# One attention block with a gate: the two loads of the gate's weights move from SyncE's queue to GpSimd's

## The chip, the cores and the metric

The kernel runs on one core of a Trainium2 chip. The metric is the device time of one execution in microseconds; before, it is 1303.49 us, the median of three runs (1303.37 to 1303.68). All data is fp32.

## The reference

One decode step for two batch rows of 512 numbers: a layer norm, attention over a cache of 32768 keys and values for 8 key heads (each shared by 4 query heads, of 128 numbers), and a gate, which is a small two-layer network on the same normed input.

```python
def reference(A_x, A_k_cache, A_v_cache, A_wq, A_wo, B_x, B_w1, B_b1, B_w2, B_b2):
    def _A_ref(x, k_cache, v_cache, wq, wo):
        ...
        q = (lambda x, *d: x.transpose(*d))((x @ wq).reshape(B, Sq, Hq, Dh), 0, 2, 1, 3)
        ...
        scores = jnp.einsum("bhqd,bhkd->bhqk", q, k) * (Dh ** -0.5)
        p = _softmax(scores, axis=-1)
        o = jnp.einsum("bhqk,bhkd->bhqd", p, v)
        ...
    def _B_ref(x, w1, b1, w2, b2):
        h = jnp.einsum("bsd,df->bsf", x, w1) + b1
        ...
        r = jnp.where(h > zero, h, zero)
        h = r * r
        out = jnp.einsum("bsf,fd->bsd", h, w2) + b2
        return out
    x = A_x
    xn = _layernorm(x, axis=-1)
    s = _A_ref(xn, A_k_cache, A_v_cache, A_wq, A_wo)
    g = _silu(_B_ref(xn, B_w1, B_b1, B_w2, B_b2))
    return x + s * g
```

The sizes: `wq` is 512 x 4096 (8.39 MB), `w1` 512 x 1792 and `w2` 1792 x 512 (3.67 MB each), `wo` 4096 x 512 (8.39 MB). Keys and values are 16 pairs of batch and key head, 16.78 MB of keys and 16.78 MB of values each.

## The kernel before

A sequence is one of the 16 pairs of batch and key head. Its keys come in two loads of 8.39 MB, its values in two more; in each, every partition gets one piece of 64 KB. Keys go into `kring`, a ring of three slots of 64 rows per partition (4.19 MB each over all partitions), values into `vbuf`, one buffer of the size of two slots. DVE transposes the keys 32 x 32 into two buffers `kt` (L309, two instructions for each slot of keys, 4.41 us each), TensorE makes scores from them (`te_scores`, L270), ACT copies the scores out, the softmax follows, and TensorE multiplies with the values (`te_values`, L280). Three hardware loops, on PE, ACT and DVE, run over the sequences 1 to 15; sequence 0 is written out ahead of them. The order on each engine is the order of the program text, and engines wait for each other by semaphores.

All big loads are issued by SyncE (`load(SP, ...)`, L84 in the profile), in the order of the text. A load that has to wait for its buffer holds up all loads behind it in that queue. Ahead of the loops the order is as follows; `transposed(q)` means that DVE is done with the q-th slot of keys.

1. `wq` into `vbuf`, which is not yet needed for values; then the first K load (two slots), then one half of the second K load (slot 2).
2. `w1` into the lower part of `vbuf`, when the query projection has read `wq` (`q_done[1]`).
3. The other half of the second K load (`k1_in`, slot 1), when slot 1 is transposed (`transposed(0)`).
4. `w2` into the upper part of `vbuf`, with the same mark as `w1`.
5. The two halves of the third K load, one after `transposed(1)`, one after `transposed(2)`.
6. The first V load, after the gate's second layer (`mlp_done`); then the fourth K load, and so on, K and V in turn.

GpSimd makes some constants in the first 2 us, then waits for the queries and makes `qz` (`set_q`, L246), the masked query that the scores of a sequence need, once for each sequence.

On TensorE and DVE the gate stands between the scores of the first slots: scores of slots 0 and 1, first layer (L375 to L378, waits for `w1`), its squared ReLU on DVE (L381 to L385), scores of slot 2 (the first half of the second K load that is used, `k1_in`), second layer (L393, waits for `w2`), scores of slot 3. DVE keeps the same order, so it transposes the keys of `k1_in` only after the first layer.

Of the kernel before, what the change touches and what calls it, by code (L numbers as in the profile page):

```python
# [11 lines left out]
P = 128  # L12
# [40 lines left out]
def gqa_decode_kernel(nc, x, kc, vc, wq, wo, w1, b1, w2, b2, out):  # L53
# [20 lines left out]
    def bank(name, n=1):  # L74
# [3 lines left out]
    SP, ACT, DVE, POOL, TE = (Lane(nc, e, n) for e, n in (  # L78
        (nc.sync, "sp"), (nc.scalar, "act"), (nc.vector, "dve"), (nc.gpsimd, "pool"), (nc.tensor, "pe")))
    tensor, vector, scalar, gpsimd, sync = nc.tensor, nc.vector, nc.scalar, nc.gpsimd, nc.sync  # L80

    def load(lane, dst, src, sem, *marks):
        lane.wait(*marks)
        return sem.after(lane.eng.dma_start(dst, src))  # L84

    def dma(name):
        return Count(nc, name, 16)
# [32 lines left out]
    def transposed(q):  # L120
        return KT[1].at(q + 1)

    def load_k_half(m, i, *marks):
        c = k_order(m)[i][1]
        return load(SP, k_slot(2 * m + i), k_rows(m)[:, c * SLOT:(c + 1) * SLOT], k_sems[m % 2], *marks)
# [7 lines left out]
    w1_t = vflat[:, 0:ND * F].rearrange("p (d f) -> p d f", d=ND)  # L133
    w2_t = vflat[:, ND * F:ND * F + FJ * D].rearrange("p (j e) -> p j e", j=FJ)
# [70 lines left out]
    q_done = []  # L205
# [5 lines left out]
                                             wq_t[:, d, cc * 512:(cc + 1) * 512], start=(d == 0), stop=(d == ND - 1)))  # L211
        q_done.append(t)

    w1_in = load(SP, w1_t, w1.rearrange("(p d) f -> p d f", p=P), dma("w1"), q_done[1])
    k1_in = load_k_half(1, 0, transposed(0))
    w2_in = load(SP, w2_t, w2.rearrange("(p j) e -> p j e", p=P), dma("w2"), q_done[1])
    load_k_half(2, 1, transposed(1))
    load_k_half(2, 0, transposed(2))

# [396 lines left out]
```

## Time and profile before

| | |
|---|---|
| median of the runs | 1303.49 us |
| span of the profiled execution | 1302.6 us |
| DVE busy | 619.0 us (48%) |
| PE busy | 639.7 us (49%) |
| ACT, GpSimd busy | 128.6 us, 11.9 us |
| read from HBM | 561.01 MB |

The span is the time from the first to the last instruction of one profiled execution; the median is of runs without a profile, and 0.9 us longer. In the profile, DMA share is the mean busy share of the core's 16 DMA engines. A row of the timeline has a start, a duration, the engine, the line in the kernel, the operation and its operands, and in brackets how long the engine was idle before and what ended that. A DMA's row on SPq or ACTq is its issue; the time at which it has landed is seen by who waits for it. The chain of work that ended last is followed back from the last instruction; a piece "DMA" in it runs from the issue to the landing.

### The profile page before, as it was taken

Reading aid. Unit: us, or ns where it says so; the run is one execution under the profiler, and the core shown is the slowest. Engines: PE = TensorE matmul, PEld = TensorE weight load, DVE = VectorE, ACT = ScalarE, POOL = GpSimd, SP = SyncE. Lnnn points to the kernel's source line nnn. Section 1 sums busy time; section 2 is a strip of 40 time slices with the busy share of each in tenths; the row PEclk is TensorE's granted clock in tenths of the full one; section 3 lists DMA queues with packets and bytes.
Section 4 is the critical chain, followed back from the end, with each engine's and each line's share of the span. In section 5 each row is a group of like instructions: output and inputs, shape, how many; then the busy total and the mean of one; then the engine's idle time right before and its main releaser. Section 6 shows DMA issues by size and latency. Waiting matters only on the chain.

```text
span 1302.6 us, 10806 instructions
## 1 busy us (share of the span) xinstructions
PE 639.7 (49%) x4710; PEld 175.6 (13%) x4710; DVE 619.0 (48%) x305; ACT 128.6 (10%) x262; POOL 11.9 (1%) x41
## 2 busy tenths in 40 slices
PE   3555444555535455544536543444653444554368
PEld 1111110111101011110101111111110111111014
DVE  2565553436555344655435555343655534455410
ACT  0111011111001011000111101011100101101010
POOL 0000000000000000000000000000000000000000
PEclk9778677878767787777788777678877778877789
DMA  9999999999999999999999999999999999999998
GB/s 419 418 448 423 441 427 435 431 437 433 431 437 427 443 427 441 429 441 427 439 427 437 433 431 437 427 443 427 441 429 441 427 439 427 439 431 429 441 425 356
DMA packets 10703, 561.14 MB, mean 431 GB/s; under 512 B 1199, under 2 KB 1219, under 8 KB 1478
## 3 DMA queue, kind: packets, MB, share of 16 engines
q1 hardware_dynamic: 10656, 560.99, 99.6%
q8 instruction: 6, 0.10, 0.0%
q10 hardware_dynamic: 38, 0.02, 0.0%
q14 instruction: 3, 0.02, 0.0%
HBM read 561.01 MB, written 0.00 MB: 431 GB/s over the span
## 4 chain that ended last, share of the span: by engine, by line
DMA 77%; DVE 12%; issue 10%; PE 1%; SPq 0%; DVEq 0%
DMA kring<-in_A_k_cache 73%; DVE kt L309 12%; DMA kring<-in_A_v_cache 2%; DMA kring<-in_A_wo 2%; PE o_ps L280 1%; PE acc_ps L533 0%; PE pj_ps L540 0%; SPq L84 0%; DVEq L308 0%; PE acc_ps L411 0%
## 5 line engine op out<-in xcount | busy, mean ns | idle before, releaser
L309 DVE STREAM_TRANSPOSE kt<-kring 128x4096 f32<-128x4096 f32 x128 | 557.6, 4414 | 449.4 <-DMA kring<-in_A_k_cache 449.4
L270 PE MATMUL ps_s<-kt,qz 128*32 128x512 f32 x2048 | 333.5, 779 | 603.4 <-DVE kt L309 603.4
L280 PE MATMUL o_ps<-vbuf,pTh 128*16 128x512 f32 x1984 | 227.5, 612 | 1.8 <-DMA vbuf<-in_A_v_cache 1.8
L270 PEld LDWEIGHTS ps_s<-kt,qz 128*32 128x32 f32 x2048 | 67.8, 128 | 845.1 <-issue 669.9
L333 ACT ACTIVATE sc<-ps_s,halves 128x512 f32<-128x512 f32 x64 | 46.6, 729 | 866.5 <-PE ps_s L270 866.5
L280 PEld LDWEIGHTS o_ps<-vbuf,pTh 128*16 128x16 f32 x1984 | 57.8, 101 | 178.0 <-issue 158.6
L343 ACT COPY pTh<-pT_ps 64x256 f32<-64x256 f32 x128 | 46.9, 366 | 39.6 <-PE pT_ps L299 21.6
L315 DVE CUSTOM_DVE_ANT_0 sc<-sc 128x1024 f32<-128x1024 f32 x16 | 19.6, 1225 | 54.9 <-ACT sc L333 54.9
L318 DVE CUSTOM_DVE_ANT_0 junk<-mx_ps,other 128x128 f32<-128x128 f32 x16 | 4.7, 292 | 82.1 <-PE mx_ps L288 82.1
L336 ACT ACTIVATE sc<-sc,nm 128x1024 f32<-128x1024 f32 x16 | 18.4, 1149 | 108.9 <-DVE nm L318 108.9
L328 DVE TENSOR_REDUCE hr<-fin_ps 128x4 f32<-128x64 f32 x16 | 3.6, 225 | 48.5 <-PE fin_ps L292 48.5
L292 PE MATMUL fin_ps<-ident,o_sb 128*128 128x128 f32 x64 | 10.5, 286 | 17.4 <-DVE o_sb L485 17.2
L348 ACT COPY o_sb<-o_ps 128x512 f32<-128x512 f32 x15 | 8.8, 586 | 97.2 <-PE o_ps L280 97.2
L299 PE MATMUL pT_ps<-ident,sc 128*128 128x128 f32 x128 | 17.5, 282 | 0.0
L299 PEld LDWEIGHTS pT_ps<-ident,sc 128*128 128x128 f32 x128 | 15.3, 147 | 0.0
L280 PE MATMUL o_ps<-kring,pTh 128*16 128x512 f32 x64 | 9.3, 749 | 9.0 <-DMA kring<-in_A_v_cache 9.0
L493 POOL COPY oT<-ho 128x4 f32<-128x4 f32 x15 | 2.8, 188 | 1147.2 <-DVE ho L329 1147.2
L210 PE MATMUL pT_ps<-vbuf,xnT 128*32 128x512 f32 x64 | 8.5, 693 | 7.4 <-DMA vbuf<-in_A_wq 7.4
L227 DVE COPY kt<-pT_ps 128x512 f32<-128x512 f32 x8 | 5.0, 683 | 13.2 <-PE pT_ps L210 13.2
L540 PE MATMUL pj_ps<-ident 128*128 128x128 f32 x88 | 10.8, 278 | 0.0
L540 PEld LDWEIGHTS pj_ps<-ident 128*128 128x128 f32 x88 | 10.1, 192 | 1.9 <-issue 1.9
L485 DVE TENSOR_TENSOR o_sb<-o_sb,o_ps 128x512 f32<-128x512 f32 x15 | 10.2, 682 | 0.0
(90 smaller groups left out, 105.5 us busy)
## 6 DMA issues: line engine op xcount, KB each, us to landing
kring<-in_A_k_cache SPq DMA_DIRECT2D x4, 4096.0 KB, 23.8
vbuf<-in_B_w SPq DMA_DIRECT2D x2, 3584.0 KB, 28.5
kring<-in_A_wo SPq DMA_DIRECT2D x1, 4096.0 KB, 41.2
kring<-in_A_wo SPq DMA_DIRECT2D x1, 2304.0 KB, 25.5
kring<-in_A_wo SPq DMA_DIRECT2D x1, 1024.0 KB, 27.6
kring<-in_A_wo SPq DMA_DIRECT2D x1, 512.0 KB, 28.4
vbuf<-in_A_v_cache SPq DMA_DIRECT2D x31, 30.1
kring<-in_A_k_cache SPq DMA_DIRECT2D x30, 29.8
```

The source lines that it names most:

```text
L270: i = tensor.matmul(ps_s[32 * g:32 * g + 32, :], qz[:, 2 * y + e, :], kt[y][:, g * NO:(g + 1) * NO, 32 * e:32 * e + 32], start=(y == 0 and ...
L280: mm_ = tensor.matmul(o_ps[32 * g:32 * g + 16, :], pTh[:, 2 * g + c, 2 * i:2 * i + 2, :, :].rearrange("p o y h -> p (o y h)"), vt[:, lo:lo ...
L292: t = tensor.transpose(fin_ps[:, i * P:(i + 1) * P], o_sb[:, i * DH:(i + 1) * DH], ident)
L299: t = tensor.transpose(pT_ps[:, k // 4, (k % 4) * P:(k % 4 + 1) * P], p[:, k * P:(k + 1) * P], ident)
L309: KT[y].after(vector.transpose(kt[y], k_slot(q)[:, :, 64 * y:64 * y + 64]))
L315: return DVE(lambda: vector.tensor_tensor_reduce(scf[0], scf[0], scf[1], 1.0, -3.4e38, ALU.add, ALU.max, rm), mark, on=on)
L333: ACT(lambda: scalar.mul(sc[c][:, :, :, u], ps_s.rearrange("p (o w) -> p o w", w=32), halves[:, c:c + 1]), *marks, on=EV)
L336: return ACT(lambda: scalar.activation(scf[0], scf[0], AF.Exp, bias=nm, scale=SCALE, accum_out=l), mark, on=on)
L343: i = scalar.copy(pTh[64 * a:64 * a + 64, :, :, y, :], v[64 * y:64 * y + 64, :, :, a0, a, :])
L348: scalar.copy(o_sb, o_ps).then_inc(OE.sem, 32)
L485: DVE(lambda: vector.tensor_add(o_sb, o_sb, o_ps), on=OSR)
L540: tensor.matmul(pj_ps[:, 0:P], ident, ident, start=True, stop=True)
```

## The change

Both loads of the gate's weights are issued by GpSimd. Their waits, sources, destinations and semaphores stay the same.

```diff
-    w1_in = load(SP, w1_t, w1.rearrange("(p d) f -> p d f", p=P), dma("w1"), q_done[1])
+    w1_in = load(POOL, w1_t, w1.rearrange("(p d) f -> p d f", p=P), dma("w1"), q_done[1])
     k1_in = load_k_half(1, 0, transposed(0))
-    w2_in = load(SP, w2_t, w2.rearrange("(p j) e -> p j e", p=P), dma("w2"), q_done[1])
+    w2_in = load(POOL, w2_t, w2.rearrange("(p j) e -> p j e", p=P), dma("w2"), q_done[1])
     load_k_half(2, 1, transposed(1))
     load_k_half(2, 0, transposed(2))
```

On SyncE, after the first K load and one half of the second, the order was this and is now this (`in_B_w1` and `in_B_w2` are the gate's weights, `kt_1` is DVE's count of transposed slots, `pe` TensorE's count of instructions done):

```order
 L84 DMA kring<-in_A_k_cache 128x16384
 L84 DMA kring<-in_A_k_cache 128x8192
-L84 DMA vbuf<-in_B_w1 128x7168 [waits pe]
-L84 DMA kring<-in_A_k_cache 128x8192 [waits kt_1]
-L84 DMA vbuf<-in_B_w2 128x7168 [waits pe]
-L84 DMA kring<-in_A_k_cache 128x8192 [waits kt_1] x2
+L84 DMA kring<-in_A_k_cache 128x8192 [waits kt_1] x3
 L84 DMA vbuf<-in_A_v_cache 128x16384 [waits pe]
 L84 DMA kring<-in_A_k_cache 128x16384 [waits kt_1]
```

The three half loads of keys that wait for DVE now follow each other with nothing between them.

On GpSimd the two loads come between its constants and the first `qz`:

```order
 L155 MEMSET ones 128x128
 L157 COPY sel4<-ident 4x128 [waits pool]
+L84 DMA vbuf<-in_B_w1 128x7168 [waits pe]
+L84 DMA vbuf<-in_B_w2 128x7168 [waits pe]
 L246 TENSOR_TENSOR qz<-qT,bm 128x128 [waits dve,act]
 L422 MEMSET oR 128x1024 [waits dve]
```

Both wait for the same count of TensorE, and `qz` stands behind them. TensorE, DVE and ACT keep their order.

## Rows read from the trace of the kernel before

**Rows 1.** of the page: span, DMA share in 40 slices, bytes, the chain's shares

```profile
span 1302.6 us, 10806 instructions
...
DMA  9999999999999999999999999999999999999998
...
HBM read 561.01 MB, written 0.00 MB: 431 GB/s over the span
...
DMA 77%; DVE 12%; issue 10%; PE 1%; SPq 0%; DVEq 0%
```

**Rows 2.** Windows: us, busy time of each engine (count), granted clock, DMA share, GB/s

```profile
40.00:100.00 60.00, 31.71 (x216) 8.95 (x216) 40.65 (x20) 8.07 (x12) 1.39 (x2) 0.73 1.01 435
100.00:1000.00 900.00, 435.93 (x3130) 109.62 (x3130) 442.48 (x194) 87.06 (x174) 6.79 (x22) 0.77 1.00 433
0.00:43.20 43.20, 13.29 (x100) 6.63 (x100) 10.77 (x25) 4.25 (x18) 1.68 (x10) 0.96 0.97 413
```

**Rows 3.** Timeline of SyncE's queue: start us, us, what (all of L84)

```profile
0.74 0.38 SPq L84 DMA_DIRECT2D vbuf<-in_A_wq  x1
...
31.55 0.33 SPq L84 DMA_DIRECT2D vbuf<-in_B_w  x1
...
52.48 0.43 SPq L84 DMA_DIRECT2D vbuf<-in_B_w  x1
...
85.66 0.33 SPq L84 DMA_DIRECT2D vbuf<-in_A_v_cache  x1
```

**Rows 4.** Chain of work that ended last: start us, us, what

```profile
43.30 8.78 DVE kt L309 x2
52.10 19.03 DMA kring<-in_A_k_cache
71.14 0.03 issue
...
71.23 8.78 DVE kt L309 x2
80.03 19.05 DMA kring<-in_A_k_cache
...
99.17 0.12 DVE kt L309
...
107.97 29.91 DMA kring<-in_A_k_cache
...
146.77 29.82 DMA kring<-in_A_k_cache
...
185.49 29.79 DMA kring<-in_A_k_cache
```

**Rows 5.** Timeline, first 48 us, engines: start us, us, what [idle before]

```profile
1.43 1.22 ACTq L84 DMA_DIRECT2D kt<-in_A_x  x1
...
10.34 0.69 DVE L188 TENSOR_REDUCE st<-kt 128x1 f32<-128x512 f32 x1 [7.33 <-DMA kt<-in_A_x]
...
22.90 8.52 PE L210 MATMUL pT_ps<-vbuf,xnT 128*32 128x512 f32 x64 [7.38 <-DMA vbuf<-in_A_wq]
...
28.12 2.48 DVE L227 COPY kt<-pT_ps 128x512 f32<-128x512 f32 x4 [12.28 <-PE pT_ps L210]
...
31.56 2.48 DVE L227 COPY kt<-pT_ps 128x512 f32<-128x512 f32 x4 [0.95 <-PE pT_ps L210]
...
35.56 0.46 POOL L246 TENSOR_TENSOR qz<-qT,bm 128x128 f32<-128x128 f32 x1 [33.58 <-ACT qT L235]
...
47.90 3.64 PE L270 MATMUL ps_s<-kt,qz 128*32 128x512 f32 x16 [12.83 <-DVE kt L309]
```

**Rows 6.** Timeline, the gate's first layer

```profile
62.64 1.01 PE L375 MATMUL pj_ps<-b1t,sel 4*128 4x448 f32 x2
...
68.56 0.65 DVE L385 STREAM_TRANSPOSE hT<-oR 128x448 f32<-128x448 f32 x1
```

**Rows 7.** Timeline, the output's store

```profile
1300.79 0.63 ACTq L587 DMA_DIRECT2D out<-fin  x1
```

## The prediction

> **What bounds the kernel now.** I read the page first, for the share of the DMA engines: its slices are full from the first to the last, 561.01 MB are read at 431 GB/s, and the chain of work that ended last is 77% DMA [rows 1]. No compute engine is above half. I then asked whether full means full in the stretch that the change touches: from 40 to 100 us the DMA share is 1.01 at 435 GB/s, and from 100 to 1000 us 1.00 at 433 GB/s [rows 2]. So the sixteen DMA engines do not rest. The kernel's time is its bytes at that rate, plus a start and a tail, and a change that leaves the bytes alone can only add idle time to the DMA engines or change their rate.
>
> The rate as a duration: one K load and one V load, 8.39 MB each, take from one K issue of the loop to the next, 146.77 to 185.49 us, 38.72 us [rows 4]. That makes 19.36 us for an 8.39 MB load, 9.68 for a half K load (4.19 MB), and 8.47 for one of the two gate weights (3.67 MB, called w1 and w2 here). These figures give the landings of the early stretch. From the first K load's landing (DVE starts at 43.30) to that of the second half of the next one (71.23), the queue moved a K half, w1 and a K half: 9.68 + 8.47 + 9.68 = 27.83 us, and the chain shows 27.93 [rows 4]. The next stretch, 71.23 to 99.17, holds w2 and two K halves: the same sum, and 27.94 shown. So a landing there can be counted from the bytes that stand ahead of it.
>
> Third, the issues of SyncE's queue. In the loop a K load is issued when DVE has transposed the keys before it; issued at 107.97 it lands 29.91 us later [rows 4], so 10.5 us of other transfers were ahead of it. That is the cushion which keeps the engines fed. It neither grows nor shrinks from turn to turn, so time that the DMA engines once lose is not won back.
>
> **The change part by part.** I name the K loads in the order in which they land: k0 (8.39 MB), k1a, k1b, k2a, k2b (halves), then v0, k3.
>
> *Issue cost.* Two issues of 0.33 and 0.43 us leave SyncE [rows 3], where the next load behind each waits for DVE anyway: nothing is gained there. They come to GpSimd, which has stood idle for 33.58 us when it starts qz at 35.56 [rows 5]. No row shows a DMA that GpSimd issues. From below it costs what SyncE needs, 0.3 us each; from above I take the longest issue of the trace, 1.22 us on ACT [rows 5], for both 2.4 us from 31.55. That ends by 34.0, before qz's inputs are there; and TensorE needs qz only when the first half of k0 is transposed, at 47.9 [rows 5]. So it costs nothing, and stays free up to some 12 us.
>
> One rule speaks against GpSimd here. The Trainium skill (SBUF — State Buffer, the section "SBUF: two separate sides") says that while VectorE runs a two-port copy, GpSimd is locked out and cannot write the descriptors of a DMA that it issues. In this stretch DVE runs eight copies of which the second four fill 31.56 to 34.04 [rows 5]. By that rule w1 would start at 34 instead of 32 to 33. The sum below would be the same by either, because it hangs on the order of the last bytes only. Those copies read PSUM, while the section's example is a copy from SBUF to SBUF.
>
> *Order of the transfers.* This is the term that matters. Before, w1 stands behind k1a, and w2 behind k1b: both take their turn in one queue. Now both are let go together at 31.55 and run beside k0 and k1a. That two queues share an engine, rather than one waiting for the other's backlog, is seen at the start: ACT's 4 KB of x, issued at 1.43, after SyncE's first load at 0.74, are used at 10.34, long before that load's 22.90 [rows 3, 5]. So w1 and w2 take part of the rate from about 33 us on. If they alternate with SyncE's rows, row by row (64 KB for k0, which is 19.36/8 = 2.42 us; 28 KB for w1, 1.06 us; estimates from the rate), k0 with some four rows per engine still to come lands about 4 us later, at 47.4. k1b, waiting for k0's first transposes (52.10 − 43.30 = 8.8 us after [rows 4]), is issued at about 56.3 instead of 52.10, and k2a at about 65. Both are still ahead of need: the bytes up to w2 and k1a last until about 70. w1 lands before 60. The gate's first layer, held up to now by TensorE's scores, gets from 62.64 to 69.21 [rows 6], 6.6 us, and is done by about 74. All this hides.
>
> k1b now is the last of the six loads, where w2 used to follow it. It lands at 71.14 + 8.47 = 79.61. DVE then transposes it, and SyncE issues k2b: that was 80.03 − 71.14 = 8.89 us [rows 4], so at 88.50. Here the cover has gone. Before, w2 and k2a lay in the queue over these 8.89 us, 18.15 us of transfers. Now k2a alone lies there, 9.68 us, and v0 is no help: SyncE reaches it after k2b, and it waits for the second layer, 5.63 us later (85.66 − 80.03) [rows 3].
>
> 9.68 against 8.89 looks like enough, but an issue is not yet a transfer. With nothing in the queue ahead, the first load, issued at 0.74, is used at 22.90 [rows 3, 5]: 22.16 us, 2.80 more than 19.36. At the end, the 4 KB output is issued at 1300.79 and the span ends at 1302.6 [rows 1, 7]: 1.8 us. So k2b lands at 88.50 + 9.68 + 1.8 to 2.8, which is 100.0 to 101.0 instead of 99.08 [rows 4]: **0.9 to 1.9 us late**. I take the middle, 1.4, since k2b is large like the first load but meets a warm queue. After it the old cushion is back: v0, issued 94.1, finds k2b under way until about 100; k3 has v0's 19.36 us ahead of it. Nothing is won back, as shown above.
>
> *Rate while two queues run.* The only stretch with two queues at work ran at 413 GB/s, 0 to 43.20, with the start in it, against 433 later [rows 2]. If the 42 us of overlap ran at 413, they would lose 42 × 20/433 = 1.9 us. From below nothing, since a share of 1.00 leaves nothing to gain. The nearer row is the x load, whose wait cost k0's queue nothing visible; I take 0, and keep 1.9 for the range.
>
> Sum: span 1302.6 + 1.4 = 1304.0. The median of the runs is 1303.49, 0.9 above the profiled span; with the same 0.9 the time is 1304.9.
>
> **The rivals.**
>
> *No gap at all.* If w1 and w2 start late or get a smaller share, so that 2 us or more of w2 land behind k1b, k1b lands earlier and w2's rest covers the gap, as today. From 33 to 79.6 us 12.8 MB of K and 7.34 MB of weights pass, so this needs a share under about a third on the average, or a start after about 41 us. Then nothing is lost: 1303.5. For it: no row shows how fast GpSimd's queue starts or how it shares. Against it: alternation row by row, which lets w2 end about 5 us ahead of k1b.
>
> *Starved weights, slower.* If GpSimd's transfers go in pieces far smaller than 28 KB while SyncE's go in 64 KB, they get a few per cent and w1 lands only when SyncE's queue runs dry. That point is 99.08 − 9.68 − 8.47 = 80.9 us. DVE's program stands at the first layer, 6.6 us, until 87.5, and only then transposes k1b, 8.9 us; k2b is issued at 96.4 and lands at 107.9 to 108.9. That is 8.8 to 9.8 us late: 1312.3 to 1313.3, about 1312.8. It decides from the share at which w1 lands after 73 us: 3.67 of the 17.3 MB that pass from 33 to 73, a fifth. For it: the x load waited 8.9 us for 4 KB, so small pieces wait for large ones. Against it: each row of w1 is 28 KB in one piece, at both ends. The Trainium skill (DMA: Bandwidth & Descriptors, section "SWDGE vs HWDGE vs iDMA") gives a packet of such a queue as preferably at most 4096 B, which, if it held for these rows, would be this case; the same page's "The descriptor swizzle" counts one descriptor per 8 KB row, which speaks for whole rows. No run here shows either.
>
> *Faster.* Only if two queues lift the rate of the early stretch: from 33 to 43 us, 10 × 20/433 = 0.5 us, 1303.0. A gain beyond that has no source in a full DMA queue.
>
> **How the numbers follow.** A repeat of this kernel can tell about 0.2% from no change, 2.6 us. Forecast (gap of 0.9 to 1.9, with or without the lost rate) 0.65, of which 0.07 lies past 2.6 us; no gap 0.17; starved weights 0.14; faster 0.04, of which 0.02 beyond 2.6 us from things that I do not see. So faster 0.02, same 0.58 + 0.17 + 0.02 = 0.77, slower 0.07 + 0.14 = 0.21. The range runs from no gap with the scatter of the runs, 1303.2, to 1302.6 + 0.9 + 1.9 + 1.9 = 1307.3; the starved case and the further tails, under 2 in 10, are left out.
>
> **What would show it.** In the trace after: k0's transposes begin at about 47 instead of 43.30; w1's matmuls begin at about 67; k1b's transposes begin at 79.7, k2b's issue stands at 88.5 and its landing near 100.5; from there every row is that much later, and the loop's period is still 38.7. A k1b that lands well before 77 speaks for the no-gap or the starved case; which of them, the start of the first layer tells (before 73, or after 80). A k0 that still lands at 43.2 means that GpSimd's queue gets little or starts late. I am wrong if the loop's own period moves, or if qz comes later than the first transposes because GpSimd is held by its issues.

## The result, and the profile after

The changed kernel takes 1306.50 us, the median of eleven runs (1306.27 to 1306.98), against 1303.66 us before (1303.37 to 1303.74, eleven runs): a ratio of 1.0023, 95% interval 1.0015 to 1.0030. It is 2.8 us slower. The forecast was 1304.9, 1.4 us slower, in a range of 1303.2 to 1307.3; the sign and the place were right and the size was half. The prediction gave 0.77 to no change, that is, to a change within 0.2%, 2.6 us; the median lies just past that mark, and the interval reaches to both sides of it.

The page of the kernel after, lines that answer to [rows 1] and the DMA queues (queue, kind, packets, MB, share of 16 engines):

```profile
span 1304.9 us, 10806 instructions
...
DMA  9999999999999999999999999999999999999998
...
q1 hardware_dynamic: 10368, 553.65, 98.2%
q0 software_dynamic: 288, 7.34, 1.3%
...
HBM read 561.01 MB, written 0.00 MB: 430 GB/s over the span
...
DMA 76%; DVE 13%; issue 10%; PE 1%; ACT 0%; DVEq 0%; SPq 0%
```

There is a new queue, with 7.34 MB in 288 packets: the two loads that GpSimd issued. The bytes are the same, and the slices of the DMA share are still all nines. A loss of 2 to 3 us is less than a tenth of a slice of 32.6 us; the page cannot show it.

Windows of the kernel after, as in [rows 2] (us, busy time of each engine with its count, granted clock, DMA share, GB/s):

```profile
40.00:100.00 60.00, 29.65 (x206) 7.42 (x206) 37.61 (x12) 3.04 (x5) 0.00 (x0) 0.75 1.00 425
100.00:1000.00 900.00, 434.24 (x3124) 111.28 (x3124) 443.04 (x200) 92.03 (x181) 8.20 (x24) 0.78 1.00 433
45.30:79.60 34.30, 16.66 (x98) 3.75 (x98) 19.61 (x7) 1.43 (x2) 0.00 (x0) 0.75 1.01 435
86.00:92.00 6.00, 5.20 (x48) 1.28 (x44) 6.00 (x2) 0.75 (x1) 0.00 (x0) 0.89 0.73 270
```

The loop runs at 433 GB/s as before, and the stretch with two queues at work, 45.3 to 79.6 us, at 435. But from 40 to 100 us the rate fell from 435 to 425 GB/s, and the last row shows where: between 86 and 92 us the engines are 73% busy. In so short a window the records, placed by their starts, make single shares rough (the next experiments show the gap sharper).

The chain of work that ended last, to be read against [rows 4] (start us, us, what; the loads have their names from the prediction, k0, k1a, k1b, k2a and k2b for the early loads of keys, v0 and k3 for the first values and the next keys):

```profile
1.18 44.08 DMA kring<-in_A_k_cache
...
45.36 8.78 DVE kt L309 x2
54.16 25.39 DMA kring<-in_A_k_cache
79.56 0.03 issue
...
79.65 17.43 DVE kt L309 x4
...
97.13 1.97 PE ps_s L270 x16
...
99.85 1.28 ACT L420
...
106.15 0.12 DVE kt L309
...
114.95 25.41 DMA kring<-in_A_k_cache
...
149.25 29.79 DMA kring<-in_A_k_cache
```

The first K load, k0, lands at 45.26 instead of 43.20. k1b lands at 79.56 instead of 71.14, and DVE takes it at 79.65. What comes next is new. Before, DVE's next wait was for k2b at 99.17. Now it begins with k2b's keys at 106.15, and this wait is not for a DMA: it ends with the softmax of the first sequence, which on DVE stands ahead of k2b's keys and had become late. k3 is therefore issued at 114.95, 7.0 us later than before, but lands at 140.36, 2.5 later than 137.88. From there every row is 2.5 us late: 149.25 for 146.77.

The issues behind it, on GpSimd and SyncE (start us, us):

```profile
31.83 1.25 POOL L84 DMA_DIRECT2D vbuf<-in_B_w  x2 [29.84 <-PE mx_ps L232]
35.56 0.46 POOL L246 TENSOR_TENSOR qz<-qT,bm 128x128 f32<-128x128 f32 x1 [2.48 <-ACT qT L235]
...
88.45 0.33 SPq L84 DMA_DIRECT2D kring<-in_A_k_cache  x1
93.89 0.33 SPq L84 DMA_DIRECT2D vbuf<-in_A_v_cache  x1
```

And two landings, each the answer of the DMA view for the one issue (KB each where known, then us from issue to landing), first k2b and then v0:

```profile
kring<-in_A_k_cache SPq DMA_DIRECT2D x1, 4096.0 KB, 11.9
...
vbuf<-in_A_v_cache SPq DMA_DIRECT2D x1, 27.1
```

The same two of the kernel before:

```profile
kring<-in_A_k_cache SPq DMA_DIRECT2D x1, 4096.0 KB, 19.0
...
vbuf<-in_A_v_cache SPq DMA_DIRECT2D x1, 32.9
```

So k2b landed at 88.45 + 11.9 = 100.35, before at 80.03 + 19.0 = 99.03: 1.3 us late. v0 landed at 93.89 + 27.1 = 120.99, before at 85.66 + 32.9 = 118.56: 2.4 us late. So by the landings the loss seems to come in two parts, 1.3 us up to k2b and another 1.1 us up to v0. The packet records show below that the second is no loss of its own.

### The profile page after: what moved, and what is told of

It reads as the page before. It is cut to its first block, busy times and chain, and to the rows that moved or that the text cites. A ratio compares the mean times of both kernels' runs of the same rounds, so it can differ in the third digit from the quotient of the medians.

```text
span 1304.9 us, 10806 instructions
## 1 busy us (share of the span) xinstructions
PE 638.4 (49%) x4710; PEld 176.3 (14%) x4710; DVE 619.0 (47%) x305; ACT 128.5 (10%) x262; POOL 13.2 (1%) x43
## 3 DMA queue, kind: packets, MB, share of 16 engines
q0 software_dynamic: 288, 7.34, 1.3%
## 4 chain that ended last, share of the span: by engine, by line
DMA 76%; DVE 13%; issue 10%; PE 1%; ACT 0%; DVEq 0%; SPq 0%
DMA kring<-in_A_k_cache 71%; DVE kt L309 12%; DMA kring<-in_A_v_cache 2%; DMA kring<-in_A_wo 2%; PE o_ps L280 1%; PE acc_ps L533 0%; PE ps_s L270 0%; ACT L420 0%; ACT sc L336 0%; DVE sc L315 0%; PE pj_ps L540 0%; ACT sc L333 0%; SPq L84 0%; DVEq L308 0%; PE mx_ps L296 0%
## 5 line engine op out<-in xcount | busy, mean ns | idle before, releaser
L270 PE MATMUL ps_s<-kt,qz 128*32 128x512 f32 x2048 | 329.0, 770 | 607.7 <-DVE kt L309 607.7
L292 PE MATMUL fin_ps<-ident,o_sb 128*128 128x128 f32 x64 | 10.5, 286 | 17.4 <-DVE o_sb L485 17.2
```

The costliest lines, as they stand in the source:

```text
L270: i = tensor.matmul(ps_s[32 * g:32 * g + 32, :], qz[:, 2 * y + e, :], kt[y][:, g * NO:(g + 1) * NO, 32 * e:32 * e + 32], start=(y == 0 and ...
L292: t = tensor.transpose(fin_ps[:, i * P:(i + 1) * P], o_sb[:, i * DH:(i + 1) * DH], ident)
```

## The experiments

Theory G: what counts is the order in which the loads land. With k1b last of the six early loads, only k2a is queued while DVE transposes k1b, and the DMA engines run dry before k2b. The rival Q: a load from GpSimd costs by itself, through a second queue on the same engines. All runs are compared with runs of the kernel before on the same chip (1303.61 to 1303.64 us).

### The order without GpSimd

The kernel before, with w2 issued by SyncE right behind w1:

```diff
     w1_in = load(SP, w1_t, ..., q_done[1])
-    k1_in = load_k_half(1, 0, transposed(0))
     w2_in = load(SP, w2_t, ..., q_done[1])
+    k1_in = load_k_half(1, 0, transposed(0))
```

> Both gate loads stay on SyncE, but w2 is issued right behind w1, ahead of the half K load k1b, so k1b lands last of the six early loads as in the changed kernel, with no load from GpSimd. Theory G (the order of the landings opens a gap: only k2a, 9.7 us, is queued while DVE transposes k1b for 8.9 us and k2b is issued): k1b lands at 79.6, k2b is issued at 88.5, time as the changed kernel, 1306.5 (1306.1 to 1306.9). Rival Q (a load from GpSimd costs by itself, by running two queues or by its slower issue): no such load, so 1303.7, as before.

Measured: 1306.41 us, ratio 1.0021 (1.0012 to 1.0030). The page's queues, the issue of k2b and DVE's start on k1b in this kernel:

```profile
q1 hardware_dynamic: 10656, 560.99, 99.4%
...
q10 hardware_dynamic: 38, 0.02, 0.0%
```

```profile
88.67 0.33 SPq L84 DMA_DIRECT2D kring<-in_A_k_cache  x1
...
79.87 17.42 DVE L309 STREAM_TRANSPOSE kt<-kring 128x4096 f32<-128x4096 f32 x4 [10.55 <-DMA kring<-in_A_k_cache]
```

No load comes from GpSimd, and the loss is all there: k1b at 79.87, k2b at 88.67. The rival Q falls. GpSimd only mattered because its queue let w2 pass k1b.

### One load at a time

Only w1 is moved:

```diff
-    w1_in = load(SP, w1_t, ..., q_done[1])
+    w1_in = load(POOL, w1_t, ..., q_done[1])
     k1_in = load_k_half(1, 0, transposed(0))
     w2_in = load(SP, w2_t, ..., q_done[1])
```

> Only w1 is issued by GpSimd; w2 stays on SyncE behind k1b. Theory G: w2 covers the issue of k2b again, k1b lands at 71.1 to 71.6, 1303.7 (1303.3 to 1304.1). Rival Q: one of two loads, half of the 2.8 us: 1305.1.

Measured: 1303.66 us, ratio 1.0000 (0.9991 to 1.0009). DVE's transposes of k1b and k2b:

```profile
71.22 17.42 DVE L309 STREAM_TRANSPOSE kt<-kring 128x4096 f32<-128x4096 f32 x4
...
99.16 13.10 DVE L309 STREAM_TRANSPOSE kt<-kring 128x4096 f32<-128x4096 f32 x3 [1.50 <-DMA kring<-in_A_k_cache]
```

k1b at 71.22 and k2b at 99.16, as in [rows 4]. A load of 3.67 MB on GpSimd, running beside k0 and k1a, costs nothing that the runs show.

Only w2 is moved:

```diff
     w1_in = load(SP, w1_t, ..., q_done[1])
     k1_in = load_k_half(1, 0, transposed(0))
-    w2_in = load(SP, w2_t, ..., q_done[1])
+    w2_in = load(POOL, w2_t, ..., q_done[1])
```

> Only w2 is issued by GpSimd; w1 stays on SyncE ahead of k1b. Theory G: k1b is last of the six loads again, lands at 79.6, the gap is as in the changed kernel, 1306.5 (1306.1 to 1306.9). Rival Q: half of the 2.8 us: 1305.1.

Measured: 1306.53 us, ratio 1.0022 (1.0013 to 1.0031), the whole loss. DVE takes k1b here at 79.89 and k2b's keys at 106.54. Of the two edits, the one on w2 is the change.

### Both on GpSimd, w2 later

The changed kernel, with w2's load behind the first qz and after the second slot of keys:

```diff
-    w2_in = load(POOL, w2_t, ..., q_done[1])
     ...
     have_q0 = set_q(0)
+    w2_in = load(POOL, w2_t, ..., q_done[1], transposed(1))
```

> Both gate loads on GpSimd as in the changed kernel, but w2 also waits for the transposes of the second key slot and stands behind the first qz in GpSimd's order, so it is issued at about 63 and runs beside k1b and k2a. Theory G: w2 ends after k1b, which lands near 74; the cover is back, 1303.7 (1303.3 to 1304.2). Rival Q: both loads still on GpSimd: 1306.5.

Measured: 1303.64 us, ratio 1.0001 (0.9992 to 1.0010). DVE takes k1b between the two other cases (this kernel's line numbers are lower by one):

```profile
75.20 17.42 DVE L308 STREAM_TRANSPOSE kt<-kring 128x4096 f32<-128x4096 f32 x4 [1.74 <-DMA kring<-in_A_k_cache]
```

Both loads are on GpSimd, their bytes are the same, and there is no loss: w2's rest is still in the queue when k1b has landed.

### The gap made longer

The changed kernel, with k2b held until the fourth slot is transposed:

```diff
-    load_k_half(2, 0, transposed(2))
+    load_k_half(2, 0, transposed(3))
```

> The changed kernel, but k2b waits for the transposes of the fourth key slot in place of the third, 8.7 us later: the gap is made longer by 8.7 us. Theory G (nothing later wins idle time of the DMA engines back): 1306.5 + 8.7 = 1315.2 (1314.7 to 1315.7). Rival C (the 10 us of transfers queued ahead in the loop absorb a later start): under 1309.

Measured: 1314.99 us (1314.86 to 1315.43, five runs), ratio 1.0088 (1.0074 to 1.0102). A window between k2a's end and k2b's first packets, and k2b's issue:

```profile
88.90:98.10 9.20, 8.09 (x68) 2.08 (x64) 8.87 (x3) 0.76 (x1) 0.00 (x0) 0.96 0.00 0
...
97.22 0.33 SPq L84 DMA_DIRECT2D kring<-in_A_k_cache  x1
```

In this window the engines move nothing at all: share 0.00. k2b is issued 8.77 us later than in the changed kernel, and the time is 8.5 us longer. The gap is real, and the loop wins nothing back.

### The gap filled with a load that nobody needs

The changed kernel and the kernel before, each with one extra load of 1.05 MB between k2a and k2b, whose data is not used (v0, which overwrites it, also waits for its landing; that line is left out here):

```diff
     load_k_half(2, 1, transposed(1))
+    pad_in = load(SP, vflat[:, 14336:16384], wo.rearrange("(p r) e -> p (r e)", p=P)[:, 0:2048], dma("pad"), q_done[1])
     load_k_half(2, 0, transposed(2))
```

> The changed kernel with one more load, 1.05 MB of wo into a part of vbuf that is free then, issued by SyncE between k2a and k2b; its data is never used, v0 overwrites it. At the loop's rate it is 2.42 us of transfers. Theory G (the DMA engines stand idle for about 2 us before k2b, and that is all that the change costs): the load fits into the idle time, 1306.05 (1305.7 to 1306.6), no slower than the changed kernel without it. Rival Q (a loss of 2.8 us that comes from the loads on GpSimd, with full DMA engines): the load adds its own time, 1308.9.

> The same extra load of 1.05 MB in the kernel before, at the same place; its data is never used. Both theories: the DMA engines are full there, so it costs its own 2.42 us: 1306.05 (1305.8 to 1306.3).

Measured: 1307.47 us (1306.77 to 1307.98) in the changed kernel, 1306.15 (1305.88 to 1306.38) in the kernel before. All eight runs of the first lie above all eleven of the second. The second is 2.5 us above the kernel before, about its own 2.42, as expected. The first is a miss: neither 1306.05 nor 1308.9. There the load cost 1.0 us (1307.47 − 1306.50) instead of 2.5, so it took up part of the gap only: the changed kernel is still 1.3 us slower than the kernel before with the same load. The issues of the extra load and of k2b, and k2b's time to landing:

```profile
63.48 0.43 SPq L84 DMA_DIRECT2D vbuf<-in_A_wo  x1
88.76 0.33 SPq L84 DMA_DIRECT2D kring<-in_A_k_cache  x1
...
kring<-in_A_k_cache SPq DMA_DIRECT2D x1, 4096.0 KB, 13.7
```

k2b is issued at 88.76 and lands at 102.5; in the kernel before with the same load it landed at 101.4. So here too 1.1 us are lost, though the extra load, issued at 63.48 and 28.6 us on its way (the DMA view of its issue), landed at 92.1, 3.3 us after k2b's issue.

Half of the extra load (columns 14336 to 15360):

> As the first of these, with half of the extra load, 0.52 MB (1.21 us), in the changed kernel. It asks why the loss is 2.8 us while k2b lands only 1.3 late. Theory G with the spread (the sixteen DMA engines come to the gap up to 1.5 us apart and leave it nearly together; the engine that later also fetches instructions, 0.97 us, ends last, and it was one of those that idled about 2 us): the small load goes into that idle time, nothing changes, 1306.5 (1306.1 to 1306.8). Theory with the last engine (the loss is what the last engine idles, 0.6 us, plus fixed 2 us at its restart): 0.6 us more, 1307.1. Rival Q: 1307.7.

Measured: 1306.50 us (1306.23 to 1307.19), ratio 1.0022 (1.0013 to 1.0031): the same time as without it, half a megabyte for nothing.

### How much cover is enough

The changed kernel with w2 cut in two; its last 7 (or 3) of 14 row blocks come from SyncE between k1b and k2a (the second layer then waits for both pieces; that line is left out):

```diff
-    w2_in = load(POOL, w2_t, ..., q_done[1])
+    w2_r = w2.rearrange("(p j) e -> p j e", p=P)
+    w2_in = load(POOL, w2_t[:, 0:7], w2_r[:, 0:7], dma("w2"), q_done[1])
+    w2b_in = load(SP, w2_t[:, 7:FJ], w2_r[:, 7:FJ], dma("w2b"), q_done[1])
```

> The changed kernel with w2 cut in two: the first half from GpSimd as before, the second (1.83 MB, 4.24 us at the loop's rate) from SyncE between k1b and k2a. The bytes are the same, and 13.9 us of transfers are queued behind k1b in place of 9.7. Theory G: the next issue comes 9.9 us after k1b's landing (8.9 us and 1 us until its first packet), 4 us before the queue is dry: no loss, 1303.7 (1303.4 to 1304.1). Rival Q (each load on GpSimd costs): 1305.8 to 1306.5, as three quarters of the bytes are still on GpSimd.

> As the other, but only the last 3 of w2's 14 row blocks (0.79 MB, 1.81 us) come from SyncE between k1b and k2a: 11.5 us of transfers behind k1b. Theory G: the queue is dry for some engines only, and the next issue arrives when little is left; the loss is part of the 2.8 us, between the 1.4 and 1.7 us that the kernels with the extra loads lost beside their own bytes and nothing: 1304.6 (1303.9 to 1305.3). Rival Q: 1306.3 to 1306.5.

Measured: 1303.79 us (ratio 1.0001, 0.9992 to 1.0010) with half of w2, 1304.74 (1.0010, 1.0001 to 1.0020) with the 3 blocks. In the first, k2b's issue and DVE on k1b (this kernel's line numbers are higher by two):

```profile
84.21 0.33 SPq L84 DMA_DIRECT2D kring<-in_A_k_cache  x1
...
75.41 17.43 DVE L311 STREAM_TRANSPOSE kt<-kring 128x4096 f32<-128x4096 f32 x4 [4.15 <-DMA kring<-in_A_k_cache]
```

Together the kernels give a table. The cover is what is queued behind k1b, at 9.68 us for k2a plus the extra bytes at the loop's rate; the loss is the time above the kernel before, less the time of bytes that this kernel moves more:

| kernel | cover, us | loss, us |
|---|---|---|
| changed kernel | 9.7 | 2.8 |
| half of the extra load | 10.9 | 1306.50 − 1303.64 − 1.21 = 1.7 |
| 3 blocks of w2 | 11.5 | 1.1 |
| the extra load | 12.1 | 1307.47 − 1306.15 = 1.3 |
| half of w2 | 13.9 | 0.2 |
| only w1 moved | 18.2 | 0.0 |

From k1b's landing to k2b's issue it is 8.89 us, so a cover of 9.7 had 0.8 to spare and lost 2.8. A spare of 3.2 still lost 1.3, and 5.0 lost next to nothing. The intervals reach about 1.2 us to either side, so neighbouring rows are not told apart (11.5 and 12.1 us of cover do not even stand in order); the two ends of the table are.

## Why the prediction was right, and its size half

**What bounds the kernel**: right. The DMA engines are full, the bytes are the same, and idle time of the engines at one place goes through to the end (8.77 us of delay gave 8.5).

**Issue cost on GpSimd**: right. Both issues took 1.25 us from 31.83, within 0.7 to 2.4, and qz ran at 35.56 as before. They ran while DVE did the second four copies of [rows 5], from 31.56 to 34.04. The Trainium skill (SBUF — State Buffer, "SBUF: two separate sides") says that GpSimd cannot write descriptors while VectorE runs a two-port copy. Whether that held anything up here no run shows: the issues were not held, but the first packets of GpSimd's queue begin at 36.34 us, after the copies, and one 64 KB packet of SyncE started on each engine in between.

**Sharing row by row**: right. The DMA view of the changed kernel from 36.2 to 43.2 us, while k0 and w1 run side by side (packets, MB, share):

```profile
q1 hardware_dynamic: 32, 2.10, 69.1%
q0 software_dynamic: 32, 0.92, 30.3%
```

32 packets of SyncE's 64 KB and 32 of GpSimd's 28 KB in the same 7 us: one of each in turn. Whole rows are the packets, and that settles the case of the starved weights. The Trainium skill (DMA: Bandwidth & Descriptors, "SWDGE vs HWDGE vs iDMA") gives a packet as preferably at most 4096 B; these rows of 28 KB were not cut to that. GpSimd's share began at about 36 us, not 33, so k0 landed at 45.3, not 47.4; w1's first layer began at 65.87, not 67. Neither mattered. The rate while two queues ran was rightly put at no loss: 435 GB/s from 45.3 to 79.6 us.

**The order of the landings**: right to a tenth. k1b was put at 79.61 and landed at 79.56; k2b's issue was put at 88.5 and stands at 88.45. The runs with one load, the late w2 and the order on SyncE alone show that this order is the cause.

**The price of the empty queue**: this is the step that failed, a term of the right kind and half the size, 1.4 us for 2.8. Read by the landing it held: 100.0 to 101.0 was written for k2b, 100.35 measured. But a load lands when the last of the sixteen DMA engines is done with its part, and the prediction counted from landing to landing, so by that engine. The others were done earlier and stood idle longer.

The packet records show it. Sixteen packets of 4 bytes end each load, each right behind a last piece of data; the DMA view counts them under 512 B. When eight or nine of the sixteen are there, half of the engines are done; "the middle engine" below means this middle of the ends. First k2a in the changed kernel, 87.00 to 87.45 us (the tenth packet is an instruction fetch):

```profile
DMA packets 10, 0.02 MB, mean 36 GB/s; under 512 B 9, under 2 KB 9, under 8 KB 9
```

Then k2b, in the kernel before (96.50 to 97.18 us) and in the changed one (99.50 to 99.82):

```profile
DMA packets 16, 0.46 MB, mean 675 GB/s; under 512 B 9, under 2 KB 9, under 8 KB 9
...
DMA packets 16, 0.52 MB, mean 1638 GB/s; under 512 B 8, under 2 KB 8, under 8 KB 8
```

And v0, in the kernel before (116.00 to 116.58) and in the changed one (118.70 to 119.18):

```profile
DMA packets 16, 0.52 MB, mean 904 GB/s; under 512 B 8, under 2 KB 8, under 8 KB 8
...
DMA packets 16, 0.52 MB, mean 1092 GB/s; under 512 B 8, under 2 KB 8, under 8 KB 8
```

The middle engine ends k2b 2.6 us late and v0 2.6 us late. So the whole loss is there at k2b, and nothing is lost behind it. Its parts: the middle engine is done with k2a at 87.44, while the last one ends at 88.78. The first packets of k2b begin at 89.39 to 90.22, the middle one at 89.54. That is 2.1 us of idle time. The first packets then take 0.6 us longer than usual (last section), together 2.7.

The other kernels agree, by the middle ends of k2b and v0 in their traces against those of the kernel before: 2.9 and 2.9 us late in the order on SyncE (runs 2.8), 2.9 and 2.9 with w2 alone (2.9), 2.9 and 2.9 with half of the extra load (2.9, its own time included), 11.4 and 11.4 with the longer gap (11.4), 1.1 and 1.1 with 3 blocks of w2 (1.1), 0.2 and 0.2 with half of w2 (0.2). With the late w2 they are 0.4 and 0.6 late, where the runs lost 0.0; its profiled execution was 0.4 us above its median. The half load was a test on record: 1306.5 was written for this reading and 1307.1 for a loss set by the last engine, and it measured 1306.50.

The landings hide this, since the last engine stands differently at each of them. The sixteen ends of one load are 1.65 to 1.9 us apart in the kernel before. After the gap all engines start nearly together, and k2b's ends are 0.44 us apart; at v0 they are 1.6 us apart again, so its landing is later by another 1.1 us. In between an instruction fetch of 16 KB took 0.97 us on one engine (from 109.44). That this fetch sets the last engine back fits, but it is not shown: the records name no engine, and no run moved the fetch.

Two smaller things stand beside the term. The median before is 1303.66 us from eleven runs, 0.2 above the 1303.49 that the sum started from. And the two profiled executions differ by only 2.4 us: the changed kernel's (span 1304.9) is among the shortest of its eleven, 1304.9 to 1305.6, while that of the kernel before (1302.6) is at the long end of 1302.0 to 1302.6, the spans of its runs beside the experiments.

**The step from trace to runs, and the chances**: that the time lies in the stated range is luck. The gap's own upper bound gave 1302.6 + 0.9 + 1.9 = 1305.4 us, and 1306.50 is past it; it is covered only by the 1.9 us for a lower rate with two queues, which did not happen. I counted only 0.07 beyond 2.6 us. With the price of the gap off by a factor of two, the 0.2% mark was inside its real uncertainty.

**A row that I had wrong**: "from there every row is that much later". DVE's start on k2b is 7.0 us late and k3's issue with it, because DVE's softmax of the first sequence became the later of two waits. v0 landed at 121.0, 6 us after k3's issue instead of the usual 10.5. The cushion took this up once and was full again at the next turn (149.25, 2.5 late).

## What to carry to other kernels

When the DMA engines are the bound, read a change of queue as a change of the order of landings: list what is still queued at each wait of the issuing engine, before and after. A wait that ended behind two loads may now end behind one, and then 9.7 us of transfers against an 8.9 us wait is a loss of 2.8 us, not a spare 0.8; here 3.2 us of spare transfers were too few, and 5.0 enough. Count the spare from the end of the middle DMA engine and not from the landing, which is that of the last one: here they were 87.44 and 88.78 us, and the loss followed the first. Test the order alone on the old queue: the same time without the new queue shows that the queue was not the cost.

## What the runs showed of the hardware

The first packets after the gap are slow. The DMA view of the changed kernel from 89.35 to 89.70 us, when k2b starts on fifteen engines:

```profile
q1 hardware_dynamic: 15, 0.49, 491.5%
```

15 packets of 32 KB took 491.5% of 16 engines over 0.35 us, 1.83 us each, where a half K load takes 9.68/8 = 1.21 us per packet. So the restart cost each of these fifteen engines 0.6 us beyond its idle time (the sixteenth started at 90.22 and took 1.25), and k2b's first packets came 0.9 us after its issue at 88.45.

And a load that is issued while another is still queued can lose all the same: with the extra load, k2b was issued 3.3 us before the landing of what stood ahead of it, and landed 1.1 us late. By the packet records the middle engine was done with the extra load at 90.16, only 1.4 us after that issue, and k2b's first packets were slow here too.
